# A transformer block in fp32: fewer and wider loads, the sink table in two parts, SP as the issuing queue, and a new order table

## The chip, the core and the metric

The kernel runs on one core of one Trainium2 chip. The core has five engines, each with an instruction queue of its own that runs strictly in order: TensorE (PE), VectorE (DVE), ScalarE (ACT), GpSimd (POOL) and SyncE (SP, which only issues transfers). The metric is device microseconds of one execution, the median of several runs.

## What is computed

Sink attention with 4 batches, 8 heads, 768 positions and head size 64 (a query sees the last 128 positions and the first 4 keys, the "sinks"), then a mixture of 4 causal attention experts over its output, of which each position takes the best 2 by a gate:

```python
scores = scale * np.matmul(q, k.transpose(0, 1, 3, 2))
keep = is_sink | in_window            # first 4 keys, or the last 128
a = softmax(np.where(keep, scores, -1e9))
x = np.matmul(a, v).transpose(0, 2, 1, 3).reshape(B, S, H * D)
logits = x @ w_gate                   # best 2 of 4 experts per position
for e in range(E):
    q, k, v = x @ wq[e], x @ wk[e], x @ wv[e]
    ye = softmax(causal(scale * (q @ k.transpose(0, 2, 1)))) @ v @ wo[e]
    out += mask_e * weight_e * ye
```

## The kernel before, in words

**Units.** A unit is one pair of heads of one batch: `first(b, hp)` for the sink attention (16 units, named "b hp 0", so 010 is batch 0, second pair) and `second(b, ep)` for a pair of experts (8 units, named "b ep 1"). 128 positions make a tile; there are 6. The first units of batch 0 (000, 010, 020, 030) are all done before the first expert unit 001 can start; from then on the first units of a batch are woven into the expert units of the batch before it.

**A first unit.** q, k and v of two heads are loaded (lines 1527 to 1545). In batch 0 PE turns q and k into head-major form (`turn_by_pe`, L1072; its steps are called "tr"); in later batches DVE does (L1090). Edge rows (tiles 0 and 1: step "both", L1115) and band rows (tiles 2 to 5: "quarters", L1133) give scores; DVE picks, masks and finds the extreme ("low", L1409 and L1471), ACT takes exponentials (L1414, L1475), POOL or ACT scales by the reciprocal sums ("norm", L1427 and L1488 on POOL, L1424 and L1486 on ACT), PE transposes (L1192), DVE or ACT evacuates (L982, L984), and PE multiplies by v (L1159). The sinks of band rows have a product of their own ("of_sinks", L1163) with a small operand `vs` that POOL makes ("spread", L1371) out of a table `vp` of all units' first four rows of v.

**The sink table** (`sink_values`, lines 935 to 958). DVE clears an 80 x 1024 area `vr` in the one buffer of tag `v2`, SP loads the 16 rows in four transfers (L943), copies them to three more places in three transfers (L948), ACT rounds the whole to `vp` (L954), POOL subtracts 16 rows (L955), and SP copies the remainder into `vp` (L957).

**Weights** (`weight`). Each is loaded (L911), rounded by ACT in pieces (L917), and POOL subtracts the remainder (L921). `wv` uses the same one `v2` buffer as the sink table, so its load waits until that is done with. The products with `wv` are step "001 mm" (L1601), the projections "proj" (L1574), the output "mm" in `store` (L1648), each output row of tiles then leaves in one transfer (L1652).

**By way of DRAM** (`by_way_of_dram`, L1285 and L1289). For some rows of expert units the probabilities are turned on DVE, written to DRAM by SP ("there"), and read back in another shape by four transfers ("back"); PE's product with them (step "av") waits for the landing.

**The order.** Nothing is scheduled at run time. `ORDER` (from line 46) gives every step a place in one long order, and for steps that two engines can do, the engine by a letter (D, A, P, S, T for DVE, ACT, POOL, SP, PE). Each engine runs its own steps in the order of these places. The numbers are places and not times. The planner's costs in the same file serve only to choose buffers and filling matmuls, as long as the table fits.

## Time and profile before

| what | us |
|---|---|
| median of 3 runs | 357.13 (356.89 to 357.67) |
| the profiled execution, its own time | 358.05 |
| span of the profiled execution, first to last instruction | 356.3 |
| busy in that span: PE, DVE, ACT, POOL | 346.4, 287.7, 282.4, 187.5 |

The views used below come from the one profiled execution. Times are us from the first instruction. A busy PE is one with a matmul in flight, which includes some waiting. A letter q behind an engine (SPq, ACTq) is its queue issuing a transfer; xN counts merged instructions; "<-" reads "written from", and in views of waits "waited for".

### The profile page before, as it was taken

The numbers are of one execution on the slowest core, as the hardware profiler recorded it, in microseconds if no ns is written. First come the engines' busy times: TensorE is split into PE (matmuls) and PEld (weight loads), VectorE is DVE, ScalarE is ACT, GpSimd is POOL, SyncE is SP. The second block draws the span as 40 slices with busy tenths as digits, with TensorE's granted clock in tenths as the row PEclk, the third lists the DMA queues.
The fourth block names the chain that finished last, engine by engine and source line by source line (L and its number), as shares of the span: only waits on it lengthen the run. The fifth ranks groups of instructions, "written<-read, shape, count | busy, mean of one in ns | idle before, by whom it ended". The sixth has DMA issues, their size and how long they took to land.

```text
span 356.3 us, 13226 instructions
## 1 busy us (share of the span) xinstructions
PE 346.4 (97%) x4756; PEld 301.9 (85%) x4756; DVE 287.7 (81%) x1255; ACT 282.4 (79%) x981; POOL 187.5 (53%) x444
## 2 busy tenths in 40 slices
PE   7899999999999999999989999999999999999995
PEld 6777899888888879988878889979898889888883
DVE  6799994999989988769798967689999883478850
ACT  2999999798999897867888857658999856476862
POOL 4589987778288233092677550274688320221600
PEclk9999999999999999999999999999999999999999
DMA  7887999644520799537985298466730491049413
GB/s 207 186 183 161 160 174 162 118 99 90 92 46 3 213 258 162 82 120 209 236 181 92 106 286 161 88 214 166 255 82 3 149 260 40 29 176 297 121 61 118
DMA packets 130849, 52.04 MB, mean 146 GB/s; under 512 B 109729, under 2 KB 125089, under 8 KB 130785
## 3 DMA queue, kind: packets, MB, share of 16 engines
q1 hardware_dynamic: 121808, 46.10, 54.2%
q10 hardware_dynamic: 8976, 5.11, 4.7%
q8 instruction: 37, 0.61, 0.8%
q14 instruction: 28, 0.22, 0.2%
HBM read 32.84 MB, written 18.09 MB: 143 GB/s over the span
## 4 chain that ended last, share of the span: by engine, by line
PE 90%; DVE 3%; DMA 2%; SPq 1%; POOL 1%; issue 1%; ACTq 0%; ACT 0%; DVEq 0%
PE b L1159 22%; PE b L1574 19%; PE b L1601 10%; PE b L1648 10%; PE b L1120 10%; PE b L1192 9%; PE b L1133 6%; PE b L1115 3%; PE b L1163 2%; DMA u<-there 1%; DMA qn<-in_q_dram 1%; SPq L1539 1%; PE b L1072 1%; DVE p L1471 1%; DVE b L1463 0%
## 5 line engine op out<-in xcount | busy, mean ns | idle before, releaser
L1345 ACT ACTIVATE p<-p,st 128x128 f32<-128x128 f32 (+5 forms) x96 | 63.5, 664 | 11.7 <-DVE st L1337 9.6
L1475 ACT ACTIVATE p<-p,st 128x132 f32<-128x132 f32 x128 | 50.6, 398 | 6.3 <-DVE st L1471 5.5
L1337 DVE CUSTOM_DVE_ANT_0 p<-b,cmask 128x384 f32<-128x384 f32 (+3 forms) x96 | 46.2, 504 | 4.3 <-PE b L1120 2.9
L982 ACT ACTIVATE pt<-b 128x256 f32<-128x256 f32 (+3 forms) x109 | 41.8, 417 | 9.4 <-PE b L1192 8.3
L1120 PE MATMUL b<-ks,qs 64*128 64x384 f32 (+3 forms) x384 | 42.8, 337 | 0.0
L1159 PE MATMUL b<-pt,vn 128*64 128x128 f32 x448 | 38.8, 280 | 0.0
L1601 PE MATMUL b<-wvh,x 128*128 128x260 f32 x192 | 36.2, 286 | 0.0
L1192 PE MATMUL b<-ident,p 64*128 64x64 f32 x760 | 36.0, 227 | 0.1
L1488 POOL TENSOR_TENSOR p<-p,st 128x528 f32<-128x528 f32 x23 | 24.5, 1068 | 19.8 <-DVE st L1180 17.9
L1192 PEld LDWEIGHTS b<-ident,p 64*128 64x128 f32 x760 | 30.0, 138 | 5.6 <-issue 2.6
L1175 POOL TENSOR_TENSOR st<-st 128x4 f32<-128x4 f32 (+1 forms) x45 | 8.8, 199 | 47.8 <-ACT p L1345 27.7
L1120 PEld LDWEIGHTS b<-ks,qs 64*128 64x128 f32 x384 | 33.1, 186 | 1.0 <-ACT pt L982 0.4
L1471 DVE CUSTOM_DVE_ANT_0 p<-b,pair_mask 128x132 f32<-128x132 f32 x128 | 32.9, 285 | 0.6
L1574 PE MATMUL b<-x,wqh 128*128 128x256 f32 (+1 forms) x128 | 32.5, 342 | 0.0
L1574 PE MATMUL b<-x,wkh 128*128 128x256 f32 (+1 forms) x128 | 32.2, 340 | 0.0
L1648 PE MATMUL b<-woh,y 128*128 128x512 f32 x96 | 32.0, 400 | 0.0
L1601 PEld LDWEIGHTS b<-wvh,x 128*128 128x128 f32 x192 | 30.1, 188 | 0.9 <-issue 0.3
L1282 DVE STREAM_TRANSPOSE u<-u 128x640 f32<-128x640 f32 (+2 forms) x36 | 29.2, 829 | 1.5 <-ACT u L991 1.4
L1414 ACT ACTIVATE p<-p,st 128x128 f32<-128x128 f32 (+1 forms) x64 | 28.5, 448 | 1.6 <-DVE st L1409 1.5
L1159 PEld LDWEIGHTS b<-pt,vn 128*64 128x64 f32 x448 | 25.2, 136 | 5.1 <-issue 2.3
L1184 POOL TENSOR_TENSOR st<-st,gate 128x2 f32<-128x2 f32 x48 | 9.1, 197 | 37.5 <-DVE st L1180 30.2
L1463 DVE COPY_PREDICATED b<-earlier,b 128x256 f32<-128x256 int32 x64 | 25.9, 421 | 2.5 <-PE b L1133 2.5
(129 smaller groups left out, 1002.2 us busy)
## 6 DMA issues: line engine op xcount, KB each, us to landing
...
```

The costliest lines, as they stand in the source:

```text
L982: nc.scalar.activation(dst(), src(), AF.Copy)
L1120: nc.tensor.matmul(o, self.qs.t[hs, a, qs], keys(hs, b), start=n == 0, stop=n == 2)
L1159: nc.tensor.matmul(o[e * 64:e * 64 + 64], lhs, rhs, start=e not in self.begun, stop=last and self.done == len(self.steps))
L1192: nc.tensor.transpose(t[g].t[:, n, :], x[gs], ident[gs, gs])
L1282: nc.vector.transpose(x(), x())
L1337: nc.vector.tensor_tensor_reduce(out=one(e)[:, cs], in0=s2[e].t[:, :(c1 - c0) * 128], in1=mask(c0, c1), scale=times, scalar=st.t[:, 3, es] ...
L1345: nc.scalar.activation(x, x, AF.Exp, bias=st.t[:, 0, es], scale=-1.0, accum_out=st.t[:, 1, es])
L1471: nc.vector.tensor_tensor_reduce(out=p.t[:, n, :], in0=s2[e].t[:, 248 * r:248 * r + SW], in1=pair_mask, scale=-scale, scalar=BIG, op0=OP.a ...
L1475: nc.scalar.activation(p.t[:, n, :], p.t[:, n, :], AF.Exp, bias=st.t[:, 0, n:n + 1], scale=-1.0, accum_out=st.t[:, 1, n:n + 1])
L1574: nc.tensor.matmul(t.t, w[a][:, c, es], X[b, c].t[:, x, cs], start=c == 0 and m == 0, stop=c == NCH - 1 and m == 2)
L1601: nc.tensor.matmul(t.t[:, :VW], X[b, c].t[:, a, qs], W["wv"][w][:, c, :], start=c == 0 and n == 0, stop=c == NCH - 1 and n == 2)
L1648: nc.tensor.matmul(t.t, Y[b, c].t[:, a, qs], W["wo"][w][:, c, :], start=c == 0 and n == 0, stop=c == EP - 1 and n == 2)
```

## The change

All loads of v fetch both heads in one transfer instead of two. k of batch 0 in units 010, 020 and 030 comes in one transfer for both heads, and the first pieces of q and k of unit 000 too. The sink table loses its clearing, its copies and its padding: it is loaded, rounded, subtracted and copied in two parts, batch 0 first (16 rows by 256) and batches 1 to 3 later (16 rows by 768), and the small operand of a unit waits only for its own part. SP issues all transfers except one piece each of q and k of unit 000 and the stores of the last batch; before, ACT also issued the rest of q of 000, q of 020, v of 000, 230 and 300, one load of `wq` and 9 stores of earlier batches. The whole `ORDER` table is new (the lines below are those that the text speaks of); the planner's model of transfers, which does not act on the chip, is new as well and left out here, as are the dependences given to it for planning.

```diff
-    " sink_values_DVE": ([7], "D"),
-    " load_SP": ([17], "S"),
-    " again_SP": ([87], "S"),
-    " sink_values_ACT": ([135], "A"),
-    " sink_values_POOL": ([145], "P"),
-    " sink_values_SP": ([185], "S"),
-    " load_SPACT": ([235, 457, 448, 349, 377, 196, 190], "SSASSSS"),
-    " weight_ACT": ([330, 292, 308, 344, 491, 486, 478, 474, 397, 436, 443, 439, 277, 243, 225, 273], "AAAAAAAAAAAAAAAA"),
-    " weight_POOL": ([364, 329, 345, 358, 495, 489, 484, 479, 415, 441, 452, 447, 298, 266, 232, 322], "PPPPPPPPPPPPPPPP"),
+    " table_SP": ([41, 103], "SS"),
+    " sink_values_ACT": ([110, 204], "AA"),
+    " rest_POOLDVE": ([132, 224], "PD"),
+    " sink_values_SP": ([147, 141, 478, 233], "SSSS"),
+    " load_SP": ([264, 483, 470, 381, 432, 162, 213], "SSSSSSS"),
+    " weight_ACT": ([322, 349, 319, 328, 507, 519, 493, 496, 438, 452, 456, 461, 419, 402, 289, 325], "AAAAAAAAAAAAAAAA"),
+    " weight_POOL": ([330, 355, 350, 343, 511, 525, 517, 501, 462, 457, 468, 475, 423, 412, 293, 368], "PPPPPPPPPPPPPPPP"),
 ...
-    "000 load_SPACT": ([1, 3, 0, 4, 16], "AASSA"),
-    "000 spread_POOL": ([210], "P"),
-    "010 tr_PE": ([29, 45, 36, 48, 181, 231, 254], "TTTTTTT"),
-    "010 norm_POOLACT": ([170, 171, 191, 183], "APPA"),
-    "220 load_SPACT": ([526, 826, 1392], "SSS"),
-    "300 load_SPACT": ([1411, 1285, 1473], "SSA"),
-    "101 by_way_of_dram_SP": ([1282, 1308, 1386], "SSS"),
-    "101 back_SP": ([1365, 1343, 1441], "SSS"),
-    "101 av_PE": ([1433, 1444, 1480], "TTT"),
-    "001 mm_PE": ([372, 383, 388, 395, 381, 386, 391, 398, 460, 467, 472, 490, 463, 482, 496, 569, 476, 485, 493, 502, 471, 480, 487, 498], "TTTTTTTTTTTTTTTTTTTTTTTT"),
-    "111 store_SPACT": ([1801, 2006, 1871, 1796, 1821, 1828], "SSAASA"),
-    "301 by_way_of_dram_SP": ([2389, 2406, 2431], "SSS"),
-    "301 back_SP": ([2414, 2437, 2462], "SSS"),
-    "301 av_PE": ([2477, 2491, 2518], "TTT"),
+    "000 load_SPACT": ([1, 3, 0, 4], "ASSA"),
+    "000 load_SP": ([19], "S"),
+    "000 spread_POOL": ([175], "P"),
+    "010 tr_PE": ([24, 30, 26, 40, 177, 226, 242], "TTTTTTT"),
+    "010 norm_POOLACT": ([157, 166, 208, 187], "PPPP"),
+    "220 load_SP": ([591, 807, 1278], "SSS"),
+    "300 load_SP": ([1408, 1175, 1491], "SSS"),
+    "101 by_way_of_dram_SP": ([1290, 1325, 1390], "SSS"),
+    "101 back_SP": ([1329, 1356, 1435], "SSS"),
+    "101 av_PE": ([1436, 1448, 1489], "TTT"),
+    "001 mm_PE": ([364, 370, 385, 392, 375, 380, 383, 388, 484, 490, 504, 509, 460, 467, 477, 497, 472, 486, 500, 506, 464, 474, 481, 494], "TTTTTTTTTTTTTTTTTTTTTTTT"),
+    "111 store_SP": ([1797, 2281, 2284, 1808, 1826, 1832], "SSSSSS"),
+    "301 by_way_of_dram_SP": ([2396, 2408, 2462], "SSS"),
+    "301 back_SP": ([2415, 2433, 2505], "SSS"),
+    "301 av_PE": ([2481, 2503, 2534], "TTT"),
 ...
-            ld = transfer(prio, many, 530, load, new=[st], fifo=tag, moves=2400 * whole / 1024)
+            ld = transfer(prio, many, 520, load, queues=(SP,), new=[st], fifo=tag, moves=2.4 * whole)
 ...
-        n = B * HP * D
-        vp, st = consts.tile([80, B * HP, D], F32R, name="vp"), buf("v2", NB * E * D)
-        vr = lambda: st.t[:80, :n].rearrange("p (b d) -> p b d", d=D)
-        def load():
-            for r in range(2):
-                for e in range(2):
-                    nc.sync.dma_start(vr()[r * 8 + e * 4:r * 8 + e * 4 + 4],
-                                      bass.AP(tensor=v.tensor, offset=v[0, e].offset, ap=[[D, 4], [2 * S * D, B * HP], [1, D]]))
-        def again():
-            for a in (16, 32, 64):
-                nc.sync.dma_start(vr()[a:a + 16], vr()[:16])
-        clear = plan.step(SINK_VALUES, {DVE: 1100}, lambda: nc.vector.memset(vr(), 0.0), (), [st], (), fifo="v2")
-        ld = plan.step(SINK_VALUES, {SP: 2000}, load, [clear], (), [st], moves=800)
-        ld = plan.step(SINK_VALUES + 0.1, {SP: 1750}, again, [ld], (), [st], moves=600)
-        h = plan.step(SINK_VALUES + 1, {ACT: 60 + 0.833 * n}, lambda: nc.scalar.activation(vp, vr(), AF.Copy), [ld], (), [st])
-        lo = plan.step(SINK_VALUES + 1, {POOL: 2430}, lambda: nc.gpsimd.tensor_sub(
-            vr()[64:80], vr()[64:80], vp[64:80].bitcast(F32)), [h], (), [st])
-        return vp, [plan.step(SINK_VALUES + 1, {SP: 460}, lambda: nc.sync.dma_start(vp[16:32].bitcast(F32), vr()[64:80]),
-                              [lo], (), [st], moves=250)]
+        vp, st = consts.tile([48, B * HP, D], F32R, name="vp"), buf("v2", NB * E * D)
+        made, rests = [], []
+        for n0, n1 in ((0, HP), (HP, B * HP)):
+            n, units = (n1 - n0) * D, slice(n0, n1)
+            raw = lambda n0=n0, n=n: st.t[:16, n0 * D:n0 * D + n].rearrange("p (b d) -> p b d", d=D)
+            def table(n0=n0, n1=n1, raw=raw):
+                for r in range(2):
+                    for e in range(2):
+                        nc.sync.dma_start(raw()[r * 8 + e * 4:r * 8 + e * 4 + 4],
+                                          bass.AP(tensor=v.tensor, offset=v[n0 // HP, e].offset, ap=[[D, 4], [2 * S * D, n1 - n0], [1, D]]))
+            def rest(units=units, raw=raw, i=len(made)):
+                (nc.gpsimd if rests[i].eng == POOL else nc.vector).tensor_sub(raw(), raw(), vp[:16, units].bitcast(F32))
+            ld = plan.step(SINK_VALUES + n0, {SP: 1300}, table, (), [] if n0 else [st], [st] if n0 else [], moves=1800 if n0 else 600, many=4)
+            h = plan.step(SINK_VALUES + n0 + 1, {ACT: 60 + 0.833 * n}, lambda units=units, raw=raw: nc.scalar.activation(vp[:16, units], raw(), AF.Copy),
+                          [ld], (), [st])
+            lo = plan.step(SINK_VALUES + n0 + 1, {POOL: 150 + 2.23 * n, DVE: 70 + 1.04 * n}, rest, [h], (), [st])
+            rests.append(lo)
+            LATER.append(ld)
+            made.append([plan.step(SINK_VALUES + n0 + 1, {SP: 560}, lambda units=units: nc.sync.dma_start(vp[32:48, units].bitcast(F32), vp[:16, units].bitcast(F32)), [h], moves=250),
+                         plan.step(SINK_VALUES + n0 + 1, {SP: 560}, lambda units=units, raw=raw: nc.sync.dma_start(vp[16:32, units].bitcast(F32), raw()),
+                                   [lo], (), [st], moves=250)])
+        return vp, made
 ...
-                            nc.tensor.matmul(t[g].t[es, c, :], nat.t[gs, lo // 2 + c // 2, e, c % 2, :], ident[gs, gs], start=True, stop=True)
+                            nc.tensor.matmul(t[g].t[es, c, :], (nat.t[gs, e, lo // 2 + c // 2, c % 2, :] if which else nat.t[gs, lo // 2 + c // 2, e, c % 2, :]), ident[gs, gs], start=True, stop=True)
 ...
-            made_vs = plan.step(prio_of(max(first, 2)), {POOL: pool_cost(256)}, spread, SINKS[1], [vs], fifo="vs")
+            made_vs = plan.step(prio_of(max(first, 2)), {POOL: pool_cost(256)}, spread, SINKS[1][number >= HP], [vs], fifo="vs")
 ...
-                    nc.gpsimd.tensor_sub(dv.t[:, d0 - 2:end - 2, e, :], x[:, d0 - v0:end - v0, e, :], x[:, d0 - 1 - v0:end - 1 - v0, e, :])
+                    nc.gpsimd.tensor_sub(dv.t[:, d0 - 2:end - 2, e, :], x[:, e, d0 - v0:end - v0, :], x[:, e, d0 - 1 - v0:end - 1 - v0, :])
 ...
-            t = buf(tag, NB // 2, 2, 2, D) if by_pe and which < 2 else buf(tag, NB, 2, D)
+            flat = by_pe and which == 1
+            t = buf(tag, 2, NB // 2, 2, D) if flat else buf(tag, NB // 2, 2, 2, D) if by_pe and not which else buf(tag, 2, NB, D) if which == 2 else buf(tag, NB, 2, D)
             nat.append(t)
             loaded.append([])
             for n, (a, z) in enumerate([(0, 2), (2, NB)] if whole and which < 2 else [(0, NB)]):
-                def load(start, t=t, src=src, which=which, a=a, z=z):
+                many = 4 if which < 2 and not by_pe else 2 if by_pe and which < 2 and z - a > 2 and not (flat and z - a == NB) else 1
+
+                def load(start, t=t, src=src, which=which, a=a, z=z, flat=flat, many=many):
+                    x = src[b, 2 * hp:2 * hp + 2]
+                    if which == 2:
+                        start(t.t.rearrange("p e t d -> p (e t) d"), x.rearrange("e (t p) d -> p (e t) d", p=128))
+                        return
+                    if by_pe:
+                        to, x = t.t.rearrange("p e m j d -> p e m (j d)") if flat else t.t.rearrange("p m e j d -> p e m (j d)"), x.rearrange("e (m p j) d -> p e m (j d)", p=128, j=2)
+                        if many == 2:
+                            for e in range(2):
+                                start(to[:, e, a // 2:z // 2], x[:, e, a // 2:z // 2])
+                        elif z - a == 2:
+                            start(to[:, :, a // 2], x[:, :, a // 2])
+                        else:
+                            start(to.rearrange("p e m x -> p (e m) x"), x.rearrange("p e m x -> p (e m) x"))
+                        return
                     for e in range(2):
-                        x = src[b, 2 * hp + e]
-                        if which < 2 and by_pe:
-                            start(t.t[:, a // 2:z // 2, e].rearrange("p m j d -> p m (j d)"),
-                                  x.rearrange("(m p j) d -> p m (j d)", p=128, j=2)[:, a // 2:z // 2, :])
-                            continue
-                        if which == 2:
-                            start(t.t[:, a:z, e, :], x.rearrange("(t p) d -> p t d", p=128)[:, a:z, :])
-                            continue
                         for h in range(2):
                             to = t.t[64 * e + 32 * h:64 * e + 32 * h + 32].rearrange("p j e d -> p (j e d)")
-                            start(to.rearrange("p (n c) -> p n c", c=32)[:, 4 * a:4 * z, :],
-                                  x.rearrange("(n r) (h c) -> h r n c", r=32, c=32)[h, :, 4 * a:4 * z, :])
+                            start(to.rearrange("p (n c) -> p n c", c=32),
+                                  x[e].rearrange("(n r) (h c) -> h r n c", r=32, c=32)[h])
                 before = [x[2][0] for x in loaded[-1]]
                 loaded[-1].append((a, z, [transfer(
-                    load_prio + (0.1 if n else 0.2 if which == 2 else 0), *((2, 550) if which == 2 else (2, 450) if by_pe else (4, 645)), load, (), [] if n else [t],
-                    [t] if n else [], moves=(240 if by_pe and which < 2 else 300) * (z - a), behind=before, fifo=None if n else tag)]))
+                    load_prio + (0.1 if n else 0.2 if which == 2 else 0), many, 530 if which == 2 else 480 if by_pe else 570, load, (), [] if n else [t],
+                    [t] if n else [], moves=(230 if by_pe and which < 2 else 400 if which == 2 else 600) * (z - a), behind=before,
+                    queues=(SP, ACT) if b == 0 and hp < 2 and which < 2 else (SP,), fifo=None if n else tag)]))
 ...
-        transfer(prio, 1, 410, lambda start: start(out[b, qs, :], o.t), [moved], (), [o], moves=650)
+        transfer(prio, 1, 400, lambda start: start(out[b, qs, :], o.t), [moved], (), [o], queues=(SP, ACT) if b == B - 1 else (SP,), moves=900)
```

## Rows read from the trace of the kernel before

**Rows 1.** Windows: stretch, length; busy PE, PEld, DVE, ACT, POOL; clock, DMA share, GB/s.

```profile
10.00:20.00 10.00, 8.67 (x282) 7.19 (x273) 8.37 (x49) 8.81 (x41) 5.79 (x14) 1.00 0.77 191
20.00:30.00 10.00, 9.13 (x231) 7.21 (x228) 10.00 (x60) 10.00 (x44) 9.49 (x19) 1.00 0.89 185
...
50.00:60.00 10.00, 10.00 (x151) 9.46 (x148) 5.75 (x30) 9.20 (x36) 7.71 (x12) 1.00 0.78 140
```

**Rows 2.** Chain of work that ended last, 40 to 48 us: start, length, what.

```profile
41.81 0.28 DVE p L1471
...
42.95 2.56 PE b L1159 x44
45.50 2.60 PE b L1601 x20
```

**Rows 3.** Groups by line and shape, 18 to 50 us, POOL: count, busy us, mean ns.

```profile
L1380 POOL TENSOR_TENSOR dv<-vn 128x256 f32<-128x256 f32 x6 | 4.3, 736 | 0.0
L1488 POOL TENSOR_TENSOR p<-p,st 128x528 f32<-128x528 f32 x4 | 4.3, 1070 | 0.3 <-DVE st L1180 0.2
...
L921 POOL TENSOR_TENSOR wvl<-v,wvh 128x260 fp32r<-128x260 f32 x4 | 2.9, 736 | 0.0
L1371 POOL TENSOR_TENSOR vs<-vp,gsel 48x256 fp32r<-48x256 f32 x4 | 2.4, 607 | 0.0
L955 POOL TENSOR_TENSOR v<-v,vp 16x1024 f32<-16x1024 f32 x1 | 2.4, 2350 | 0.1
```

**Rows 4.** Groups by line and shape, 18 to 50 us, ACT.

```profile
L1486 ACT ACTIVATE p<-p,st 128x132 f32<-128x132 f32 x12 | 3.9, 408 | 0.0
...
L917 ACT ACTIVATE wvh<-v 128x260 fp32r<-128x260 f32 x4 | 1.7, 420 | 0.0
...
L954 ACT ACTIVATE vp<-v 80x1024 fp32r<-80x1024 f32 x1 | 1.1, 1051 | 0.0
```

**Rows 5.** Groups by line and shape, 18 to 50 us, DVE.

```profile
L1471 DVE CUSTOM_DVE_ANT_0 p<-b,pair_mask 128x132 f32<-128x132 f32 x30 | 7.7, 281 | 0.0
...
L984 DVE COPY pt<-b 128x256 f32<-128x256 f32 x8 | 3.2, 416 | 0.2 <-PE b L1192 0.2
```

**Rows 6.** Groups by line and shape, whole span, DVE.

```profile
L1045 DVE TENSOR_TENSOR qs<-b,qs 128x512 fp32r<-128x512 f32 x8 | 5.5, 690 | 2.2 <-ACT qs L1042 2.0
```

**Rows 7.** Timeline of DVE, 3.8 to 7 us.

```profile
4.09 0.91 DVE L951 MEMSET v<- 80x1024 f32 x1 [0.16 <-issue]
```

**Rows 8.** Chain of work that ended last, 0 to 14 us.

```profile
2.20 3.79 DMA qn<-in_q_dram
...
11.09 0.66 issue
```

**Rows 9.** Timeline of PE, 187 to 188 us: in brackets the idle time before.

```profile
187.24 0.98 PE L1159 MATMUL b<-u,v 128*64 128x128 f32 x14 [1.33 <-DMA u<-there]
```

**Rows 10.** Timeline of SP (its issues), 174 to 190 us.

```profile
174.55 0.34 SPq L1285 DMA_DIRECT2D there<-u  x1
174.99 1.36 SPq L1535 DMA_DIRECT2D vn<-in_v_dram  x2
176.53 4.93 SPq L1539 DMA_DIRECT2D qn<-in_q_dram  x4
181.51 1.94 SPq L1289 DMA_DIRECT2D u<-there  x4
```

**Rows 11.** SP's waits, 174 to 190 us.

```profile
SPq L1539 <- DMA vn<-in_v_dram: 4.0, 1, 4.0
```

**Rows 12.** DMA view: issues, KB each, median us from issue to landing.

```profile
there<-u SPq DMA_DIRECT2D x6, 512.0 KB, 3.8
```

**Rows 13.** SP's waits, whole span.

```profile
SPq L1285 <- DVE u L1282: 67.2, 14, 21.0
```

**Rows 14.** Timeline of SP, 24 to 36 us.

```profile
34.48 0.51 SPq L911 DMA_DIRECT2D v<-in_moe_w_gate_dram  x1
```

**Rows 15.** Timeline of ACT, 36.9 to 38 us.

```profile
37.29 0.43 ACT L917 ACTIVATE wvh<-v 128x260 fp32r<-128x260 f32 x1
```

995 lines of the change are left out of this document (507 added, 488 removed).

## The prediction

> **What bounds the kernel now.** I read the windows first, to see where PE is the full engine and where others are; then the chain of work that ended last, to see what hands over at the border; then the groups of the first 50 us, to price steps; last the waits of PE, to find stalls after that border. From 20 to 30 us DVE and ACT are busy 10.00 of 10 and POOL 9.49, while PE runs 231 matmuls with holes; from 50 to 60 us PE is full and DVE has dropped to 5.75 [rows 1]. So the kernel has two regimes: up to about 45 us the vector engines set the time, after it PE does. The chain shows the border: DVE's masking steps until 42 us, then products of PE, and at 45.50 the first product with `wv`, from which PE goes on in a dense row of work [rows 2]. What PE has to do after 45.50 is hardly changed: the same steps, and, counted over both tables, 185 changes between kinds of PE step in each. A change of the time has to come from an earlier first `wv` product, or from a stall of PE behind it.
>
> **The first 45 us.** In the table that product moves from place 372 to place 364, with the same 58 PE steps up to it and other steps of the vector engines. Counted over both tables, the steps ahead of it go from 48 to 45 on POOL, 105 to 101 on ACT and 139 to 136 on DVE.
>
> POOL loses the remainder of the whole sink table (2.35), three weight remainders that now come later (3 x 0.74 = 2.2) and one step of differences (2 x 0.74 = 1.5). It gains the remainder of the first part, 256 columns instead of 1024 (an estimate by columns, 0.59), a spread (0.61) and two scalings of at most 1.07. That is 6.05 against 3.3: 2.7 less [rows 3].
>
> ACT loses two weight roundings (2 x 0.42) and a scaling in four pieces (a third of 3.9, so 1.3). The rounding of the sink table, 1.05 before, stays the same amount in two pieces, with perhaps 0.2 for the second start [rows 4]. Four evacuations come from DVE, at DVE's duration some 1.7. Two splits, an exponential and a short scaling leave as well, which I put at 0.4 each from the instructions around them. The sum is about 1.8 less.
>
> DVE loses the four evacuations (4 x 0.42) [rows 5] and gets the remainder of the second part, 16 x 768. The trace has no such instruction; the nearest is the subtraction of 128 x 512 at 0.69 [rows 6], by columns 1.0. The other score steps that change sides (four leave, five come) cancel within 0.4. The net is 0.7 less. The clearing of the table (0.91) is gone too, but it ran at 4.09, before the second piece of q was there, and so gives nothing [rows 7, 8].
>
> All three engines are full, so the one that is relieved least decides: 0.7, of DVE. The bounds of this are 0 (the new order opens holes as large) and 2.7 (POOL decides).
>
> Ahead of that lie the first transfers. The chain waits 3.79 for the landing of q and again 0.66 at 11.09, where PE stands in the middle of turning k of unit 010 [rows 8]. After the change that k is one transfer, and q of 020, v of 000 and the sink table come behind it. The last transfer of the first unit is issued one issue (0.45) earlier, because q and k now have three each on two queues; but PE now turns the second pieces of both before the first scores, which takes that back, so I count nothing for it. Of the 0.66 I take 0.6: between 10 and 20 us DVE is busy only 8.37 [rows 1], so earlier scores find room. Bounds 0 and 0.66. The two table loads cost SP eight transfers where there were four and three copies; they stand behind the loads of units 000 to 020 and the small operand of unit 000 is made at place 175 instead of 210. I cost this at nothing, covered by POOL's other work; if the copies land late, POOL stands with its scalings, at worst what it has gained.
>
> Together the first regime gives 1.3 (0 to 3.4).
>
> **The stall at 187 us.** Here PE waits 1.33 for a landing of probabilities read back from DRAM [rows 9]. SP's timeline says why: the write to DRAM goes at 174.55, then SP issues a v and four transfers of a q, the latter over 4.93 instead of some 2, and only at 181.51 the read back [rows 10]. 4.0 of that is a wait of the q transfers for a landing of v [rows 11]. In the new table that v (unit 220) is at place 1278, long before the write at 1390; the q (unit 300) still stands at 1408 between it and the read back at 1435. With the v gone the four q transfers take their 2 us and end by about 177. The write has landed 3.8 after its issue, at 178.7 [rows 12]; the read back then starts nearly 3 us earlier than 181.51 and the data lie there before PE comes. So all 1.3 goes, and the next in line is PE's own order. Bounds 0 and 1.33. ACT also drops three issues of v in that stretch; PE does not wait for ACT alone there, so I give nothing.
>
> **Everything on SP.** ACT's 25 issues become 6. After 50 us PE covers ACT, so this is worth nothing by itself; for SP it is 19 issues more from ACT and 4 more for the sink table, and 21 fewer by the merged v, k and first pieces. SP stood 67.2 in all before its writes to DRAM, waiting for DVE's turned data [rows 13], so it has the time. In unit 301 the third write now stands behind the second read back, and PE's product with it comes three steps later in PE's order; I cost it at nothing, and at up to 1.33, the one such stall of before, if PE's other work is no cover [rows 9].
>
> **Sum.** -1.3 -1.3 = -2.6 on the profiled execution's 358.05. That execution is 0.92 above the median of 357.13, so I take the same off: **354.5 us**. A measurement of this kernel can tell about 0.2% (0.7 us) from no change.
>
> **The rivals.**
>
> DVE stands behind POOL. The remainder of the second part is the one DVE instruction of the first stretch with both inputs in SBUF, and it starts while POOL is nearly always inside an instruction. If it has to wait for the end of one, up to a scaling of 1.07 [rows 3], DVE's gain of 0.7 is lost and a little more: 354.5 + 1.1 = 355.6. [...] Chance 0.12.
>
> The stall at 187 stays, because four transfers of q are still ahead of the read back and wait for another landing. Then only the first regime gains: 358.05 - 1.3 - 0.92 = 355.8. Chance 0.10.
>
> Neither gain: the holes of a new order eat 1.3 in the vector stretch and the stall moves to another read back. 357.1. Chance 0.11.
>
> More than forecast: POOL, not DVE, decides the first stretch, and its 2.7 comes through with the 0.66. 354.5 - 2.1 = 352.4. For it speaks that POOL is nearly as full; against it that the chain goes through DVE [rows 2]. Chance 0.08.
>
> Slower: `wv` comes late. Its load stands behind the second part of the sink table, whose copy must land first (they share a buffer), and moves from place 235 to 264. Before, its last transfer was issued at 34.48 + 0.51 [rows 14] and the first rounding ran at 37.29 [rows 15], 2.3 later. If SP keeps the pace of the places (372 places in 45.50 us), the load moves by 3.5 us, the first rounding to 40.8, and with one rounding (0.42) and four remainders (4 x 0.74) the first product can be at 44.2: just where I have it. Every further hold of SP then delays PE one for one. One of 4.0, as the one above, puts the product at 48.2, 2.7 later than before; less the 1.3 of the stall the time is 358.05 + 2.7 - 1.3 - 0.92 = 358.5. It turns to slower when the load lands 2.6 us or more behind that pace. Against it: SP has the same 36 issues ahead of `wv` as before, with ACT's share down from 8 to 3, and no more bytes. Chance 0.19.
>
> **How the numbers follow.** The forecast has 0.40; with the three rivals below 356.4 (0.12, 0.10, 0.08) faster is 0.70, same 0.11, slower 0.19. The range goes from 351.8, a little below the case with POOL, to 358.2, which is short of the slower case by 0.3: half of that case's chance lies above, and with a tenth for what I have not thought of about 2 in 10 are left out.
>
> **What would show it.** Right: the first `wv` product at about 44.2, DVE and ACT at 10 of 10 from about 13 us on, no wait of PE for "u<-there" near 187, and from the first product on a PE as dense as before. The early step is wrong if PE still waits on k of 010 near 11 us; the POOL and DVE steps are wrong if the product starts at 45.5 or later with DVE full; the stall step is wrong if a wait of over 1 us for a read back appears anywhere. Wrong altogether: ACT or POOL idle before a `wv` rounding (late load), or POOL idle before a spread (late copies).

## The result, and the profile after

The changed kernel takes 361.96 us (median of 10, 360.56 to 362.83) against 357.81 for the kernel before in the same comparison (10 runs): a ratio of 1.0103, 95% interval 1.0075 to 1.0132. It is slower, where 354.5 was forecast, and it lies above the range. The profiled execution happens to be the fastest of its ten: 360.56 with a span of 358.7, against 358.05 and 356.3 before.

To see where the time went I count PE's work: every kind of product at its own dense pace (the usual step from one to the next of its kind), products of zeros left out, the same total in both kernels. The lag is the time at which a kernel has done a given amount, less the time at which the kernel before had done it; more lag is later. Four profiles (e1 is the changed kernel again, e7 and e3 are runs below; worked out from all matmul rows, times and lags in us):

| kernel before at | 19.6 | 34.1 | 47.0 | 58.0 | 68.0 | 78.8 | 185.4 | 198.1 | 250.1 | 349.5 |
|---|---|---|---|---|---|---|---|---|---|---|
| changed | -0.2 | -0.8 | -0.1 | 1.0 | 1.0 | 2.7 | 2.9 | 1.3 | 2.2 | 2.9 |
| changed, e1 | 2.6 | 2.1 | 2.8 | 3.9 | 3.9 | 5.6 | 5.8 | 4.2 | 5.2 | 5.9 |
| e7, q and k by head | -1.2 | -2.1 | -1.3 | -0.2 | -0.2 | 1.6 | 1.9 | 0.2 | 1.1 | 1.9 |
| e3, before with v of 220 early | 0.3 | 0.3 | 0.3 | 0.2 | 0.2 | 0.6 | 0.6 | -0.5 | -0.5 | -0.7 |

So something is won before 34 us, given back by 58, some 1.7 more is lost between 68 and 79, some 1.6 comes back around the stall at 187, and 1.6 trickles away behind it. The two executions of the same changed kernel differ by 2.8 at 20 us and by nearly the same 3.0 at the end.

The windows after, in the columns of [rows 1]:

```profile
10.00:20.00 10.00, 8.23 (x273) 7.25 (x263) 8.15 (x52) 8.34 (x39) 5.64 (x14) 1.00 0.79 189
20.00:30.00 10.00, 9.37 (x238) 7.61 (x234) 9.16 (x60) 9.86 (x44) 9.02 (x18) 1.00 0.62 123
...
50.00:60.00 10.00, 9.59 (x144) 8.63 (x144) 6.68 (x33) 9.75 (x40) 7.65 (x13) 1.00 0.56 110
```

DVE and POOL are no longer full from 20 to 30 us, as their relief should show; but from 50 to 60 PE has lost its density and ACT is as good as full. The chain, 0 to 16 us, answers to [rows 8], and its part from 40 to 48 us to [rows 2]:

```profile
1.85 4.79 DMA kn<-in_k_dram
...
10.87 0.72 issue
15.20 1.05 issue
```

```profile
42.02 0.91 ACT p L1438 x2
...
44.59 1.35 ACT p L1489 x7
```

The first landing in the chain comes at 6.64 (6.00 before), the wait near 11 us is still there, and a second one is longer (0.38 before). The chain at the border goes through ACT's steps, not DVE's. PE's timeline (L1626 is L1601 of before, L1173 is L1159, L1129 is L1115):

```profile
45.35 0.39 PE L1626 MATMUL b<-wvh,x 128*128 128x260 f32 x1
...
50.50 1.02 PE L1129 MATMUL b<-kx,qn 64*128 64x128 f32 x8 [0.41 <-ACT pt L996]
...
188.94 1.04 PE L1173 MATMUL b<-u,v 128*64 128x128 f32 x16
```

The first `wv` product is where it was (45.43 before); the product with the probabilities read back carries no idle time now, where [rows 9] had 1.33, but it also comes 1.7 later (188.94 for 187.24). The timelines of DVE and POOL near 77 us show what [rows 5] had nothing of:

```profile
76.45 0.20 DVE L1660 RECIPROCAL gate<-gate 128x6 f32<-128x6 f32 x1
76.68 1.70 DVE L1661 TENSOR_TENSOR gate<-gate 128x24 f32<-128x24 f32 x1
78.30 0.68 DVE L1351 CUSTOM_DVE_ANT_0 p<-b,cmask 128x512 f32<-128x512 f32 x1
```

```profile
76.35 0.61 POOL L1385 TENSOR_TENSOR vs<-vp,gsel 48x256 fp32r<-48x256 f32 x1
76.92 1.42 POOL L1394 TENSOR_TENSOR dv<-vn 128x256 f32<-128x256 f32 x2
```

A DVE multiplication of 24 columns (median 0.18 in this profile) lasts until POOL's subtraction of unit 100 ends, and the masking step whose bank PE wants starts only then. In the kernel before, the longest of the same five small steps there takes 0.45.

### The profile page after: what moved, and what is told of

Its sections match the earlier page's. It is cut to its first block, busy times and chain, and to the rows that moved or that the text cites. A ratio compares the mean times of both kernels' runs of the same rounds, so it can differ in the third digit from the quotient of the medians.

```text
span 358.7 us, 13226 instructions
## 1 busy us (share of the span) xinstructions
PE 348.5 (97%) x4772; PEld 301.3 (84%) x4772; DVE 284.4 (79%) x1243; ACT 280.2 (78%) x980; POOL 190.6 (53%) x449
## 4 chain that ended last, share of the span: by engine, by line
PE 82%; DVE 6%; ACT 4%; DMA 2%; issue 2%; POOL 1%; SPq 1%; ACTq 0%; POOLq 0%
PE b L1173 20%; PE b L1599 17%; PE b L1673 10%; PE b L1626 9%; PE b L1134 8%; PE b L1206 7%; PE b L1147 6%; PE b L1129 3%; DVE p L1351 2%; DMA kn<-in_k_dram 2%; PE b L1086 1%; PE b L1177 1%; ACT p L1489 1%; SPq L1562 1%; ACT p L1428 1%
## 5 line engine op out<-in xcount | busy, mean ns | idle before, releaser
L1359 ACT ACTIVATE p<-p,st 128x384 f32<-128x384 f32 (+5 forms) x96 | 63.5, 664 | 11.2 <-DVE st L1351 9.8
L1351 DVE CUSTOM_DVE_ANT_0 p<-b,cmask 128x384 f32<-128x384 f32 (+3 forms) x96 | 45.3, 504 | 1.3 <-PE b L1134 0.7
L1173 PE MATMUL b<-pt,vn 128*64 128x128 f32 x448 | 39.1, 280 | 0.0
L1189 POOL TENSOR_TENSOR st<-st 128x2 f32<-128x2 f32 (+1 forms) x45 | 8.8, 196 | 54.1 <-ACT p L1359 41.1
L1502 POOL TENSOR_TENSOR p<-p,st 128x528 f32<-128x528 f32 x26 | 27.7, 1066 | 15.9 <-ACT p L1489 6.5
L1626 PE MATMUL b<-wvh,x 128*128 128x260 f32 x192 | 35.9, 285 | 0.0
L1428 ACT ACTIVATE p<-p,st 128x256 f32<-128x256 f32 (+1 forms) x64 | 28.8, 450 | 4.2 <-DVE st L1423 4.1
L1626 PEld LDWEIGHTS b<-wvh,x 128*128 128x128 f32 x192 | 29.9, 188 | 1.0 <-issue 0.5
L1173 PEld LDWEIGHTS b<-pt,vn 128*64 128x64 f32 x448 | 25.4, 136 | 5.9 <-issue 3.1
```

The source lines that it names most:

```text
L1173: nc.tensor.matmul(o[e * 64:e * 64 + 64], lhs, rhs, start=e not in self.begun, stop=last and self.done == len(self.steps))
L1351: nc.vector.tensor_tensor_reduce(out=one(e)[:, cs], in0=s2[e].t[:, :(c1 - c0) * 128], in1=mask(c0, c1), scale=times, scalar=st.t[:, 3, es] ...
L1359: nc.scalar.activation(x, x, AF.Exp, bias=st.t[:, 0, es], scale=-1.0, accum_out=st.t[:, 1, es])
L1428: nc.scalar.activation(x, x, AF.Exp, bias=st.t[:, 0, n:n + 1], scale=-1.0, accum_out=st.t[:, 1, n:n + 1])
L1626: nc.tensor.matmul(t.t[:, :VW], X[b, c].t[:, a, qs], W["wv"][w][:, c, :], start=c == 0 and n == 0, stop=c == NCH - 1 and n == 2)
```

## The experiments

All times are medians; a ratio is to the kernel before, measured beside the run on the same chip. Five groups were each measured together: e1 to e4, e5 to e8, e9 to e12, e13 to e16, and e17 with e18. The kernel before had medians of 357.82, 357.25, 357.52, 358.02 and 358.09 there, so small differences between runs of two groups say little.

The planner also fills gaps of PE with products of zeros, and an edit can change their number. Every kernel has 12 at its start. Beyond these the kernel before has none, the changed one 16, e2 20, e5 60, e8 48, e13 32, and e6, e14, e17 and e18 none.

| run | median | ratio, 95% interval |
|---|---|---|
| e1 changed kernel again | 362.79 | 1.0112 (1.0060 to 1.0163) |
| e2 differences of 100 later | 361.38 | 1.0101 (1.0071 to 1.0130) |
| e3 before, v of 220 early | 356.93 | 0.9972 (0.9946 to 0.9998) |
| e4 evacuations of 000 to DVE | 363.55 | 1.0128 (1.0067 to 1.0189) |
| e5 SP ahead of the copies | 365.00 | 1.0202 (1.0170 to 1.0234) |
| e6 no zeros | 362.88 | 1.0139 (1.0105 to 1.0173) |
| e7 q, k by head | 360.51 | 1.0091 (1.0057 to 1.0125) |
| e8 q, k of 020 later | 365.28 | 1.0210 (1.0183 to 1.0236) |
| e9 e7, gate earlier | 362.59 | 1.0119 (1.0076 to 1.0162) |
| e10 before, q, k merged | 358.68 | 1.0031 (1.0012 to 1.0050) |
| e11 before, v merged | 359.21 | 1.0033 (1.0010 to 1.0055) |
| e12 e7, evacuations of 030 | 360.67 | 1.0078 (1.0049 to 1.0107) |
| e13 before, v of 010 early | 361.33 | 1.0091 (1.0063 to 1.0119) |
| e14 e6, k of 020 later | 361.95 | 1.0110 (1.0083 to 1.0136) |
| e15 e7, copy for differences | 359.70 | 1.0067 (1.0026 to 1.0107) |
| e16 e3, v of 000 later | 357.29 | 0.9970 (0.9946 to 0.9994) |
| e17 e7, v of 000, k of 020 later | 360.24 | 1.0068 (1.0039 to 1.0097) |
| e18 e5 without zeros | 362.21 | 1.0153 (1.0087 to 1.0219) |

**The changed kernel again.**

> The changed kernel once more, nothing edited, so that the next three can be read against it on the same chip and a second profile of it is there. If its loss is built into its order, a gate multiplication of about 1.7 us stands again near 76.7 us, the read-back of unit 101 is met without a wait near 188 us, and the time is 361 to 363 us. If the 1.7 us was a chance of the one profiled execution, it is missing or below 0.5 us here, and the profiled span is about 1.2 us shorter than 358.7.

The 1.68 us multiplication is there again (79.58 us), and the time agrees. What differs is the start, in PE's timeline:

```profile
13.90 0.40 PE L1086 MATMUL b<-ident,kn 64*64 64x64 f32 x11 [3.11 <-issue]
```

The wait of 0.72 is 3.11 here. That became the first open question. It is not the whole difference: soon behind it TensorE's granted clock is 0.50, from 14.5 to 17.9 us. From 15 to 17 us, in the columns of [rows 1], the first profile and e1:

```profile
15.00:17.00 2.00, 0.95 (x30) 0.80 (x28) 1.65 (x14) 0.82 (x4) 1.08 (x2) 1.00 0.60 162
```

```profile
15.00:17.00 2.00, 2.00 (x54) 2.00 (x50) 0.47 (x2) 0.92 (x6) 0.28 (x1) 0.50 0.07 20
```

Both profiles have the same matmuls in the same order. At the 223rd e1 is 2.3 behind, at the 340th, after the half clock, 3.9, and at the 349th 2.7, because there the first profile has its second wait and e1 has none. Such a stretch stands in e1, e4, e9 and e18, and in none of the other 16 profiles ahead of the last stores. A long wait alone does not bring it: e6 waits 2.67 and keeps 1.00.

**The stall at 187 us alone.**

```diff
-    "220 load_SPACT": ([526, 826, 1392], "SSS"),
+    "220 load_SPACT": ([526, 826, 1278.5], "SSS"),
```

> The kernel before with one place changed: v of unit 220 goes out ahead of the read-back of unit 101, as in the changed kernel. Theory 1 (the whole 1.33 us wait near 187 us comes from SP standing for that buffer): the wait is gone and the kernel is 1.2 to 1.6 us faster than the kernel before. Theory 2 (the wait only moves, to the buffer that v takes or to the DMA): less than 0.4 us gained, with a new wait on v or on the read-back between 180 and 200 us.

Theory 1 holds in its cause; the gain is below its range. SP's and PE's timelines:

```profile
175.14 0.34 SPq L1285 DMA_DIRECT2D there<-u  x1
177.12 3.43 SPq L1539 DMA_DIRECT2D qn<-in_q_dram  x4
180.68 1.87 SPq L1289 DMA_DIRECT2D u<-there  x4
```

```profile
186.70 1.09 PE L1159 MATMUL b<-u,v 128*64 128x128 f32 x16 [0.21 <-DMA u<-there]
```

The read back goes out at 180.68, only 0.8 earlier than in [rows 10]: q holds SP until 180.55, and the write, issued at 175.14, has landed only at 180.61 by the chain, after 5.47. Of the 1.33 a wait of 0.21 is left, and the lag falls by 1.1 between 185 and 198 us. In the medians it is 0.9. This kernel beats both, with an interval that just leaves out 1.

**The gate step beside POOL: three runs.** The first puts the subtraction behind the first step that needs the gate.

```diff
-    "100 differences_POOL": ([629], "P"),
+    "100 differences_POOL": ([644.5], "P"),
```

> The changed kernel with the differences of unit 100 on POOL one step later, behind the first step that needs the gate, so that DVE's gate multiplication does not meet them. Theory 1 (DVE stood 1.5 us behind POOL's subtraction, and PE behind DVE): the multiplication takes 0.18 to 0.25 us, and the kernel is 1.0 to 1.5 us faster than the unedited one of this call. Theory 2 (PE has other work or is late for another reason there): the multiplication is short, but the time changes by less than 0.3 us, and a wait of about the same length stands at the next products of unit 100.

The multiplication is 0.18 again (the step two ahead of it takes 0.62 now, beside POOL's spread), and against the profile of the unedited kernel 0.57 us are won by 81 us; but at 82.23 PE then waits 0.43 for a scaling of POOL that now stands behind the subtraction, and by 100 us only 0.15 is left. The trace goes with theory 2. The medians do not: e2's is 1.41 below that of e1, as theory 1 has it, and 0.58 below the first ten of the changed kernel. As the start alone moves e1's profile by 2.8, four executions of e1 cannot settle it. (Its span of 361.2 has a last store that landed some 2.2 late; e7's has the same.)

The second moves the gate's steps instead, on top of e7:

```diff
-    "001 values_ACT": ([615], "A"),
-    "001 weigh_DVE": ([624], "D"),
+    "001 values_ACT": ([596], "A"),
+    "001 weigh_DVE": ([597], "D"),
```

> The changed kernel with q and k of the first batch loaded head by head (the run before this), and with the gate's exponential and weighing of batch 0 moved up on ACT and DVE by seven and nine steps, into a stretch in which POOL does nothing with two operands in SBUF for 1 us. In the run before, one of DVE's five small gate steps stood for 1.86 us near 75 us. Theory 1 (that stand is what PE loses there): none of the five is above 0.4 us, the loss against the kernel before between 70 and 85 us (1.8 us in the run before) falls by 1.0 to 1.5 us, and the time with it. Theory 2 (the order of that stretch is late in another place as well): the stand goes and the loss falls by less than 0.5 us.

Both missed, to the worse side: two of the five steps still stand (0.64 and 0.79), and PE waits for the masking steps that come later:

```profile
75.66 1.68 PE L1134 MATMUL b<-ks,qs 64*128 64x512 f32 x6 [1.38 <-DVE st L1351]
```

From 68 to 79 us it loses 4.0 where e7 loses 1.8. But part of this is the clock. Soon behind the wait of 1.38 it is 0.50, from 76.1 to 79.5 us, where e7 has 1.00:

```profile
76.50:79.00 2.50, 2.50 (x20) 1.69 (x17) 2.19 (x10) 2.04 (x8) 1.91 (x4) 0.50 0.00 0
```

The one execution of e9 with a mean clock of 1.000 took 360.17, the three at 0.993 to 0.995 took 362.46 to 363.08. So what the move costs at the full clock is not settled. The third leaves the order alone:

```diff
-  nc.gpsimd.tensor_sub(dv.t[:, d0 - 2:end - 2, e, :], x[:, e, d0 - v0:end - v0, :], x[:, e, d0 - 1 - v0:end - 1 - v0, :])
+  (nc.gpsimd.tensor_copy(dv.t[:, d0 - 2:end - 2, e, :], x[:, e, d0 - v0:end - v0, :]) if number == HP else
+   nc.gpsimd.tensor_sub(dv.t[:, d0 - 2:end - 2, e, :], x[:, e, d0 - v0:end - v0, :], x[:, e, d0 - 1 - v0:end - 1 - v0, :]))
```

> The changed kernel with q and k of the first batch head by head, in which the differences of unit 100 are not computed: POOL copies v instead, in the same place, with one operand instead of two (the output of this unit is another). Theory 1 (a subtraction of two SBUF operands on POOL keeps out DVE's gate step of two): each of the five gate steps near 75 us takes 0.4 us or less instead of 1.86 us, and the loss of 1.8 us between 70 and 85 us falls by 1.0 us or more. Theory 2 (the gate step waits for something else): it is still over 1 us. Theory 3 (the stand is real, but PE has to wait in this order anyway): the gate steps are short and the loss falls by less than 0.5 us.

DVE's gate steps in e7 and in this run (L1660 here is L1659 there), and POOL's copy:

```profile
74.98 1.85 DVE L1659 TENSOR_SCALAR gate<-gate 128x6 f32<-128x6 f32 x1
```

```profile
75.12 0.65 DVE L1660 TENSOR_SCALAR gate<-gate 128x6 f32<-128x6 f32 x1
```

```profile
75.35 0.73 POOL L1394 COPY dv<-vn 128x256 f32<-128x256 f32 x2
```

PE's loss from 68 to 79 us falls from 1.84 to 0.66, while the stand falls by 1.20, and 1.1 stays to the end of the profile. So here the stand costs PE nearly its length. The copy is also shorter than the subtraction (0.73 for 1.40), and DVE still stood 0.46 beside it and the spread ahead of it; so the run shows that POOL's step holds DVE and what that costs, not that the second operand is what does it.

**Evacuations.** First four of unit 000, then two of unit 030 on top of e7, from ACT to DVE:

```diff
-    "000 fn_DVEACT": ([..., 122, 127, 120, 118, 145, ...], "DDDADADAAAAAAAAADA"),
+    "000 fn_DVEACT": ([..., 122, 127, 120, 118, 145, ...], "DDDADADAADADDDAADA"),
...
-    "030 fn_DVEACT": ([...], "ADDDAADDDADADAADDA"),
+    "030 fn_DVEACT": ([...], "ADDDAADDDADADDADDD"),
```

> The changed kernel with four evacuations of unit 000 given back from ACT to DVE (those at places 85, 118, 120 and 127, about 0.4 us each on ACT), as in the kernel before. Theory 1 (ACT, full from 20 to 60 us, gives up there what the change won): ACT idles 1 us more between 20 and 60 us and the kernel is 0.5 to 1.2 us faster than the unedited one of this call. Theory 2 (DVE is as full in this stretch, so it pays what ACT saves): no gain, between -0.3 and +0.8 us.

> The changed kernel with q and k of the first batch loaded head by head, and with two evacuations of unit 030 (about 0.3 us each at 50 us on ACT) given to DVE, which idles 3 us of the 10 behind 50 us. PE waited there for sk and pt of ACT (0.87 and 0.41 us). Theory 1 (ACT, full from 40 to 55 us, sets this stretch): both waits shrink, and 0.4 to 0.8 us are gained against the run with split loads alone. Theory 2 (PE is held by something behind it as well): less than 0.2 us gained.

Against e1, whose start is alike (waits of 3.11 and 2.71, then the half clock), e4 loses 0.5 by 34 us and keeps it: ACT idles 1.9 from 20 to 30 us, DVE is fuller (9.80 for 9.39), and the end is later. So relief of ACT gains nothing there and load on DVE costs: of the two it is DVE that PE follows, as forecast, though four evacuations of some 0.4 cost only 0.5. In e12 the wait at 50 us grows:

```profile
51.24 1.02 PE L1129 MATMUL b<-kx,qn 64*128 64x128 f32 x8 [0.63 <-ACT woh L929]
```

The two evacuations come behind a transposition of 0.57 on DVE. From 47 to 58 us e12 loses 1.4, e7 1.1. So ACT alone is not what holds this stretch; the full queue on either side is. The row's ACT release fits no evacuation there, so what PE waited for last is not settled.

**SP's stand before the copies (the slower rival).**

```diff
-        ... buf("v2", NB * E * D)
+        ... buf("u", NB * E * D)
-    " sink_values_SP": ([147, 141, 478, 233], "SSSS"),
-    " load_SP": ([264, 483, 470, 381, 432, 162, 213], "SSSSSSS"),
-    "020 load_SP": ([7, 23, 156], "SSS"),
+    " sink_values_SP": ([157, 163, 478, 266], "SSSS"),
+    " load_SP": ([214, 483, 470, 381, 432, 140, 213], "SSSSSSS"),
+    "020 load_SP": ([7, 23, 139], "SSS"),
```

> The changed kernel with the table of sinks in a buffer that nothing else needs before 70 us, and with wv, one piece of wo and v of unit 020 issued on SP ahead of the copies of the table instead of behind them, so that SP stands for the copies with less behind it. Theory 1 (the rival of the prediction: SP's stand before the copies, 4.5 us at 17.38 and 2.85 us at 28.54, makes wv late and with it the first product at 45.35 us): that product starts 0.5 to 1.3 us earlier and the kernel is 0.5 to 1.3 us faster than the unedited one. Theory 2 (ACT and DVE are full up to 45 us, so an earlier wv waits for its turn): wv lands 5 us or more earlier, the first product stays within 0.3 us of where it stands against the work before it, and the time within 0.4 us.

> The run with the table of sinks in its own buffer and wv, wo and v of unit 020 ahead of the copies on SP, once more, without any products of zeros (that run had 44 more of them than the changed kernel, 2.8 us of PE's time). Theory 1 (SP's stand before the copies makes the first products late): counted from 20 us on, PE is 0.5 to 1.3 us further by 50 us than in the changed kernel without zeros, and the median is 361.6 to 362.4 against 362.9 us. Theory 2 (wv had to wait for its turn on ACT and POOL in any case): PE is within 0.3 us of it by 50 us, and the median within 0.5 us.

e5 can't be read: the planner put 44 more products of zeros on PE at 27 to 31 us. Without any (e18) it can, from 20 us on; before that PE has a wait of 2.52 for its first pieces, where e6 has 0.89, and then the half clock, from 8.0 to 11.4 us. SP's timeline of the changed kernel, then of e18:

```profile
15.88 1.50 SPq L957 DMA_DIRECT2D v<-in_v_dram  x4
21.89 0.60 SPq L970 DMA_DIRECT2D vp<-v  x1
...
31.39 0.52 SPq L970 DMA_DIRECT2D vp<-v  x1
...
35.27 2.25 SPq L923 DMA_DIRECT2D v<-in_moe_wv_dram  x4
```

```profile
27.26 2.09 SPq L923 DMA_DIRECT2D v<-in_moe_wv_dram  x4
```

SP does stand, 4.5 us ahead of 21.89, and `wv` goes out 4.1 later than before (35.27 for 31.16). But 8.0 earlier buys nothing: from 20 to 47 us e18 keeps its distance to e6 (0.6 and 0.7). By the trace theory 2 holds. The median of 362.21 fits the range of theory 1, but e6 is of another group, and against the kernel before the two ratios (1.0153 and 1.0139) do not differ.

**The products of zeros.** `FILL_END` is set to 0, and the 16 products are gone.

> The changed kernel without the 16 products of zeros that it puts on PE at 38.1 us (the kernel before has none there); nothing else is changed, and they write to a bank that is overwritten. If they stand in the way of the products behind them, 0.5 to 1.0 us is gained; if they only fill time in which PE would wait, less than 0.2 us, and a wait of about 0.9 us shows in their place.

Nothing is gained in the median, and from 34 to 68 us the lag is that of the changed kernel within some 0.1: they fill time in which PE waits (0.55 for POOL at 38.74). Behind 198 us this profile has one wait of 0.99 more, for the evacuation of an output row.

**The start: what PE waits for.** Loads by head again, then q and k of unit 020 later:

```diff
-  many = 4 if ... else 2 if by_pe and which < 2 and z - a > 2 and not (flat and z - a == NB) else 1
+  many = 4 if ... else 2 if by_pe and which < 2 else 1
...
-    "020 load_SP": ([7, 23, 156], "SSS"),
+    "020 load_SP": ([30, 45, 156], "SSS"),
```

> The changed kernel with q and k of the first batch loaded head by head again (two transfers each, as before), all else as changed. The second profile of the changed kernel stood 3.1 us for k of unit 010, which it loads in one transfer of 384 KB; the first stood 0.7 us. Theory 1 (the one large transfer is what lands late): the wait at 11 to 14 us falls to 0.7 us or less, and the median is 1 to 2 us below that of the unedited kernel. Theory 2 (what is issued beside it, q and k of unit 020, takes the DMA engines from it): the wait stays between 0.7 and 3.1 us and the median within 0.5 us.

> The changed kernel with q and k of unit 020 issued behind v of unit 000 and behind the first part of the table of sinks (they go out at 4.4 and 7.4 us in the changed kernel; before, q went out at 5.4 and k at 10.5 us). Theory 2 of the run with split loads (they take the DMA engines from k of unit 010): k lands 1 to 3 us earlier, the wait at 11 to 14 us is below 0.7 us, and the median is 1 to 2 us below that of the unedited kernel. Theory 1 (the size of the one transfer): the wait stays between 0.7 and 3.1 us, and the median within 0.5 us.

e7's median is 2.4 below that of e6, measured beside it; against the kernel before, its interval and those of e1 and of the first ten overlap. Its first landing is over 1 us earlier (PE waits 0.27 for it, where the two profiles of the changed kernel have 1.25 and 1.55), and with it the first product:

```profile
11.08 0.40 PE L1086 MATMUL b<-ident,kn 64*64 64x64 f32 x11 [1.03 <-issue]
...
44.12 0.39 PE L1626 MATMUL b<-wvh,x 128*128 128x260 f32 x1
```

The landing varies with the execution, but the difference is there in all of them together: in the new order PE goes on behind its first pieces at 6.0 to 7.5 us with merged loads (nine profiles, median 6.61) and at 5.6 to 6.5 with split ones (five, median 5.84). But the wait stays, 1.0 here, 1.7 in e12, 3.0 in e9, all with split loads. e8 got 32 products of zeros at 12 us, so its time says nothing of the loads. Neither theory was right, and the trace says why: in all 15 profiles that have a wait at 10 to 14 us (that of the kernel before is one of them) PE stands before the same matmul, the 223rd, and goes on 1.3 to 1.6 us after a packet of the queue called "instruction" has landed. It is that packet, in the DMA view of e1 from 11 to 12 us and of the changed kernel's first profile from 8 to 9 us (packets, MB, share):

```profile
q8 instruction: 1, 0.02, 7.4%
```

```profile
q8 instruction: 1, 0.02, 6.5%
```

The times from the traces (PE's 97th matmul; packet; end of the 222nd; start of the 223rd):

```
kernel      97th   packet         222nd ends  223rd
before      7.74   9.21 - 10.42   11.09       11.75
e3          8.69   9.70 - 10.88   no wait
e16         8.82   8.44 -  9.52   no wait
e13         7.38   9.51 - 10.70   11.48       12.23
changed     7.45   8.99 - 10.04   10.87       11.59
e1          7.37  11.35 - 12.53   10.80       13.90
e6          6.75  10.20 - 11.52   10.21       12.88
e7          6.46   8.48 -  9.55   10.05       11.08
e9          6.60  10.24 - 11.55   10.02       13.06
e14         7.45  10.36 - 11.61   10.88       13.03
e17         6.42   7.91 -  8.92   no wait
e18         8.55   9.89 - 10.86   no wait
```

The next stand, where there is one, is always before the 349th: 126 matmuls on, with 126 weight loads beside them, and there too PE goes on 1.2 to 1.6 us after a packet of that queue. The 349th is a product of scores in the kernel before and a transposition of probabilities in the changed one, so it is the count that decides, and not a product or its data. I read this as PE waiting for its own code, and the expectations below call it that. No run took a packet away, so none shows it, but the count, the packet and the missing releaser all point to it. Two runs in each kernel then moved data out of or into its way: in the kernel before, v of 010 early (e13) and v of 000 later (e16, on top of e3); in the changed one, k of 020 later (e14, on top of e6), and v of 000 as well (e17, on top of e7 without zeros).

```diff
-    "010 load_SPACT": ([5, 8, 68], "SSS"),             e13
+    "010 load_SPACT": ([5, 8, 9], "SSS"),
-    "000 load_SPACT": ([1, 3, 0, 4, 16], "AASSA"),     e16
+    "000 load_SPACT": ([1, 3, 0, 4, 40], "AASSS"),
-    "020 load_SP": ([7, 23, 156], "SSS"),              e14
+    "020 load_SP": ([7, 45, 156], "SSS"),
-    "000 load_SP": ([19], "S"),                        e17
+    "000 load_SP": ([45], "S"),
-    "020 load_SP": ([7, 23, 156], "SSS"),
+    "020 load_SP": ([7, 46, 156], "SSS"),
```

> The kernel before with one place changed: v of unit 010 (384 KB) goes out on SP at about 5.2 us instead of 11.7 us, when nothing needs it yet. In all twelve profiles of this study in which PE stands at 10 to 14 us it stands before the same instruction (the 223rd of PE that is recorded) and goes on 1.3 to 1.6 us after the same 16 KB packet of the queue called instruction has landed. Theory 1 (PE waits for its own code, and the packet stands behind the data that was issued before it): the packet, at 9.2 to 9.7 us in the kernel before, comes 0.5 us or more later, PE's wait grows to 1 us or more, and the median is 0.5 to 1.5 us above that of the kernel before. Theory 2 (PE waits for k of unit 010 or for another load that the profile does not show): the packet's time has nothing to do with it, and the median stays within 0.3 us.

> The changed kernel (without the products of zeros) with k of unit 020 issued behind the first part of the table of sinks, at about 10 us as in the kernel before, instead of at 7.4 us. Theory 1 (PE's code packet stands behind the data): the packet comes at 9.0 us or earlier (8.5 to 11.4, 9.9 in the mean, in the nine profiles that issue this load early), PE's wait there is 1 us or less, and the median is 0.5 to 1.5 us below the 362.9 us of the run without zeros. Theory 2: no change within 0.5 us, or slower for want of k.

> The kernel before with v of unit 220 ahead of the read-back (the run that gained 0.9 us) and with v of unit 000 issued on SP at about 9.8 us instead of on ACT at 6.4 us. Theory 1 (less data ahead of PE's code packet): the packet comes at 8.7 us or earlier, PE does not wait at 11 us, and the median is 0.2 to 0.7 us below that run. Theory 2: within 0.2 us of it, or slower by what v then comes late.

> The changed kernel with q and k of the first batch head by head and without the products of zeros, in which v of unit 000 and k of unit 020 are issued behind the first part of the table of sinks, so that 768 KB less stand in the DMA queues while PE's second code packet is wanted. In the kernel before, the same step with v alone brought the packet from 1.0 us behind PE's entry into the block ahead of it to 0.4 us before it. Theory 1 (what is issued early holds the code back): the packet comes within 1 us of that entry, PE does not wait at 10 to 13 us, and the median is 0.5 to 2 us below the 360.5 us of the run with split loads. Theory 2 (something else of the changed order holds it): it comes 2 us or more behind the entry, and nothing is gained; v of unit 000 comes late for its products at 16 us in either case if it lands after 15.5 us.

The 97th matmul is 126 ahead of the 223rd, as the 223rd is of the 349th; e17's expectation calls such a stretch a block. From PE's 97th matmul to the packet it takes 0.4 to 1.5 us in the kernel before and e3, e10, e11, and -0.4 with less data (e16), 2.1 with more (e13). In the changed order 12 profiles have 1.5 to 4.0, 2.7 in the mean; e14, one of them, has 2.9. In e17, where the wait is gone, it is 1.5, in e18 1.3, with a wait at the 349th alone. In the old order the direction is that of theory 1. In the new one e14 goes against it, and e18 has no wait though it moves neither load: its PE ran at the half clock there and came to the 223rd late. So e17's missing wait can't be put down to the loads either. e13's packet moved less than expected (9.51 for 9.21) and the wait grew by 0.1; its 3.3 us say nothing of it, for the planner put 32 products of zeros at 17.93 us, and the lag is -0.3 at 18 us and 1.7 at 19. e16 gains nothing over e3, which has no wait either, and misses its range. e14's median lies 0.9 below that of e6, of another group, as forecast, but its packet came at 10.36 and not at 9.0 or earlier. e17 won little over e7: PE met the next packet of that queue, 12.58 to 13.74, with a stand of 1.06 before the 349th matmul, and was at 19.6 where e7 was. What orders the packet among the data stays open.

**The merged transfers in the old order.** The loading code of the change for q and k of batch 0 (e10), and for v of all units (e11), put into the kernel before, places and queues as they were:

```diff
e10 ...
+                        if z - a == 2:
+                            start(to[:, :, a // 2], x[:, :, a // 2])
+                        elif flat and z - a == NB:
+                            start(to.rearrange("p e m x -> p (e m) x"), x.rearrange("p e m x -> p (e m) x"))
e11 ...
+                    if which == 2:
+                        start(t.t.rearrange("p e t d -> p (e t) d"), src[b, 2 * hp:2 * hp + 2].rearrange("e (t p) d -> p (e t) d", p=128))
+                        return
```

> The kernel before, its order and queues kept, with the change's transfers for q and k of the first batch: both heads in one for the first pieces and for all of k. Theory 1 (the large transfers are what lands late in the changed kernel): 0.7 to 2.5 us slower than the kernel before, lost before 16 us. Theory 2 (they are late only with everything on one queue): within 0.5 us of the kernel before.

> The kernel before, its order and queues kept, with both heads' values in one transfer of 384 KB instead of two of 192 KB, in all units. The prediction gave this part nothing. If that holds, within 0.5 us of the kernel before; if the large transfer hurts as that of k does, 0.5 to 2 us slower, lost before 20 us; SP stands about 7 us less for issuing either way.

Each makes the kernel before slower by about 0.3%, with intervals that leave out zero: 1.1 us (0.4 to 1.8) and 1.2 us (0.4 to 2.0). In e10 PE waits 1.32 at 6.60 us for the first pieces (0.38 and 0.31 before, and it goes on at 5.7 to 6.0 us in all five other profiles of the old order), but catches up by 20 us in the one profile; e11's profile has 0.9 before the 349th matmul (0.38 before) and a lag of 0.3 at 20 us and 0.6 at the end. The one profile of each does not show where the whole of the median's loss lies.

## Why the prediction was wrong, step by step

**The early wait, -0.6: wrong, and misread.** The step said that PE stands at 11.09 in the middle of turning k of 010, and that its one transfer would end that. The row said "issue", which means that nothing the profile shows was waited for; by count and packet I read it as a wait for PE's code, and one transfer for k did not end it. The wait is 0.7 and 3.1 in the two profiles of the changed kernel; their difference at 20 us, with the half clock in it, stays to the end almost whole. Whether that is why nine of the ten executions are slower than the profiled one no run shows, since only profiled executions show their start. The first landing, which the step put at par, is 0.6 later (6.64 for 6.00).

**Wider transfers for nothing: wrong.** Merged q and k cost 1.1, merged v 1.2, in the old order. The prediction counted their issues on SP and put their landings at nothing without a reason.

**The first regime, -0.7: earned, then given back.** With the start mended (e7) PE is 2.1 ahead at 34 us, and the first `wv` product starts at 44.12, where 44.2 was forecast; with the changed kernel's own start it is 45.35 and, in e1, 48.26. That DVE decides there, and not ACT, is what e4 shows up to 34 us; from 40 to 48 us the chain of the changed kernel goes through ACT. The step that failed is "from which PE goes on in a dense row of work" and "what PE has to do after 45.50 is hardly changed". Equal counts of changes between kinds of step said nothing of waits: from 34 to 58 us even e7 loses 1.9, at places like 50.50, where PE waits for an evacuated bank. No run shows what all of this is made of. The lower bound of this term, holes as large as the gain, was the right one.

**DVE behind POOL: the right mechanism at the wrong place.** The rival looked at the remainder of the table on DVE. That it waits for POOL no run shows: it took 0.94 at 30.43, for 1.0 by its columns, and there it was POOL that stood, 0.82 for a step of 0.22. The price, 1.1, came true by luck: it was worked out from a scaling of 1.07 and a gain that is lost, and what PE lost was a stand behind two subtractions of 0.7. The place was the gate's five small steps, which the first 45 us don't contain; the rival should have been carried through the kernel for every DVE step that may meet POOL.

**The stall at 187, -1.3: right in its cause.** It is gone; by itself it is worth 0.9 to 1.1 (e3), because the write took 5.47 to land and not the 3.8 of the step. The step has the read back "nearly 3 us earlier than 181.51". In the changed kernel it goes out at 181.21, 0.3 earlier by the clock:

```profile
176.52 0.34 SPq L1299 DMA_DIRECT2D there<-u  x1
179.09 2.02 SPq L1562 DMA_DIRECT2D qn<-in_q_dram  x4
181.21 1.90 SPq L1303 DMA_DIRECT2D u<-there  x4
```

PE is 2.7 late there, so for PE it comes 3.0 earlier. The q transfers take their 2 us, as the step has it.

**Everything on SP, 0: right for `wv`, open otherwise.** The forecast's slower rival named a late `wv`. It did go out 4.1 late, and e18 shows that this did not matter. The sign was the rival's, the cause was not.

**Not foreseen:** 1.6 between 198 us and the end, in pieces of 0.1 to 0.3 at many places; half of it, 0.8, is lost by 222 us. Profiles e1, e2, e7 and e17 lose the same there, so it is built into the order. No run was made on it.

As a rough sum against the +4.1 of the medians: the two merges +2.3 (measured in the old order, so only roughly additive), POOL's hold +1.1 and the stall -1.1 (from profiles). The remaining 1.8 no run takes apart: it holds the first regime's gain, what is lost from 34 to 58 us, the spread of the start, and the trickle at the end. e3 (0.9972) and e16 (0.9970) are faster than both kernels; between the two there is no difference.
